# Forgetting attention and a gated convolution FFN: the second load of the gates on the sync engine's queue, and another order for the first quarter of the work

## The chip, the core and the metric

The kernel runs on one core of a Trainium2 chip. The metric is the device time of one execution in microseconds (us); the time given for the kernel is the median of several runs. A core has five engines that each work through their own list of instructions in order and wait for one another through semaphores: PE (TensorE, matmuls; its weight loads are shown as PEld), DVE (VectorE), ACT (ScalarE), POOL (GpSimd) and SP (SyncE, which here only issues DMA transfers). ACT can issue DMA transfers too; each of the two has a DMA queue of its own.

## The reference

```python
# q, k, v: (8, 8, 576, 64) = batch, heads, sequence, head dim; f: (8, 8, 576)
scores = (q @ k.T) / sqrt(64)
cum = cumsum(log(clip(f, 1e-4, 1)), axis=-1)
scores = where(causal, -1e9, scores + cum[..., :, None] - cum[..., None, :])
attn = softmax(scores) @ v
x = attn.transpose(0, 2, 1, 3).reshape(8, 576, 512)
h = relu(x @ w_in)                        # (8, 576, 1024)
conv = conv_w[0] * h[t - 1] + conv_w[1] * h[t] + conv_w[2] * h[t + 1]
out = (h * sigmoid(conv)) @ w_out         # (8, 576, 512)
```

## The kernel before

**Groups and blocks.** The 64 heads are worked in 16 groups of 4 (`hb` 0 to 15); two groups make one batch entry (`b` 0 to 7), whose feed-forward part (FFN) starts when both of its groups are through. Keys come in blocks of 128 and one of 64.

**Tasks.** Every piece of work is a named task. `Plan.add` records its engine, what it needs, and which buffers it takes and gives back; `Plan.play` emits the tasks in the order of the string `ORDER`, one name after another. That string therefore sets each engine's list: a task stands on its engine behind all tasks of that engine that are ahead of it in the string, and where a task may run on several engines, `@ACT`, `@DVE` or `@POOL` behind its name chooses. Nothing is reordered afterwards.

The names that matter here (first number: the group, the pair of heads, or the batch entry):

- `ld0.p.s`, `ld1.p.s` (L159): plain loads of q (s = 0) and k (s = 1) of groups 0 and 1; `tp` (L166): their transposes on PE, 9 each; `cl` (L172 on ACT, L174 on DVE): the copy of a transpose out of PSUM into the working tile `qk`. Its scale and bias also clear the rows between and set the constant ones that stand beside the decay rows.
- `q2.s` and on (L180): for groups 2 and later q and k are loaded by a transposing DMA, in one go per side; `cl2.s` and on (L186) then clear the rows between on DVE, up to group 7.
- `dca` (L527), `dcl` (L267), `dcs` (L271), `dck` (L274, L275): clip f, its logarithm, the running sum, and the decay rows `kc` in bfloat16, as a high and a low part. Partitions 0 to 63 hold the 64 heads, and 64 to 127 hold them again, so f is loaded twice, from L223 and L224. `ki` (L280) writes the rows to a DRAM image in three stores; `rw1` and on (L203, L204) load them from there into the tile of a group. Group 0 does not need that image: its scores add the decay with two more matmuls (L316, L318).
- `cw`, `cwt` (L295, L298 to L305): the convolution weights, transposed on PE, and their ratios.
- `sd`, `so` (L313, with L321 for the mask): the diagonal and off-diagonal scores of a pair of heads; `st`: the tail of a group; `ed`, `eo` (L354, L371), `et` (L333): their exponentials on ACT.
- `v` (L210): loads of v in five pieces per batch entry; `va` (L218, L220): the cast to float16; `pv` (L390, L395): attention times v; `n`, `m` (L404, L406): the normalisation on DVE; `t` (L415) and `tx` (L418): the transposed result `xt`.
- `wi`, `wic`, `wo`, `woc` (L511, L519): loads of w_in and w_out in four pieces each through the tiles `ob`, and their casts.
- `f` (L430): first FFN matmul of a slice of 128 features; `r` (L441): its relu on ACT; `c`, `d` (L447, L449): the two steps of the convolution on DVE; `a` (L452): the gate's tanh or sigmoid on ACT; `g` (L459): the product on DVE; `o` (L475): the second FFN matmul; `e`, `s`: its way out.

Matmuls and transposes write to four PSUM tiles in turn (`ps0` to `ps3`), so a task on PE can also wait for the engine that empties the tile that it takes.

**Queues.** All loads and stores but three are issued by SP. ACT issues the two loads of f and the load of the convolution weights (L226) at the very start. A DMA on SP waits until the one that used the same one of eight completion semaphores has landed; those show as `DMAHW0` to `DMAHW7` in the order below.

## Time and profile before

| what | us |
|---|---|
| runs shown | 249.43, 246.55, 248.5; median 248.5 |
| the profiled execution's own time | 246.53 |
| its span, first to last instruction | 244.8 |
| PE busy | 226.9 |
| DVE busy | 205.9 |
| ACT busy | 206.8 |
| POOL busy | 51.5 |

The clock that TensorE was granted is 0.999 over the span. A profile row of a group gives the engine, the line, the operation, what it writes and reads with the form, its busy time and its mean; a row of the timeline gives the start, the length, the engine and line, and in brackets how long the engine was idle before and what ended that. The chain of waits follows the work that ended last back from the end; its rows give the start, the length and who held the chain. `SPq` and `ACTq` are the engines as issuers of DMAs; such a row lasts as long as the issue, not as the transfer.

### The profile page before, as it was taken

The numbers are of one execution on the slowest core, as the hardware profiler recorded it, in microseconds if no ns is written. First come the engines' busy times: TensorE is split into PE (matmuls) and PEld (weight loads), VectorE is DVE, ScalarE is ACT, GpSimd is POOL, SyncE is SP. The second block draws the span as 40 slices with busy tenths as digits, with TensorE's granted clock in tenths as the row PEclk, the third lists the DMA queues.
The fourth block names the chain that finished last, engine by engine and source line by source line (L and its number), as shares of the span: only waits on it lengthen the run. The fifth ranks groups of instructions, "written<-read, shape, count | busy, mean of one in ns | idle before, by whom it ended". The sixth has DMA issues, their size and how long they took to land.

```text
span 244.8 us, 6395 instructions
## 1 busy us (share of the span) xinstructions
PE 226.9 (93%) x2627; PEld 145.2 (59%) x2627; DVE 205.9 (84%) x323; ACT 206.8 (84%) x278; POOL 51.5 (21%) x77
## 2 busy tenths in 40 slices
PE   0899799779989999999999999999999999999991
PEld 0787585557555676575556765685575566444440
DVE  5635359999998999999999979996999889999941
ACT  2768677999989899999999999999988996798442
POOL 8020520004220030022311580165302221000000
PEclk9999999999999999999999999999999999999999
DMA  7999999999899999999999999969997870541426
GB/s 189 333 162 243 289 212 197 196 249 260 187 178 177 222 162 246 252 297 208 195 251 264 202 189 274 263 144 186 240 255 192 210 165 3 146 162 58 163 86 214
DMA packets 120280, 49.68 MB, mean 203 GB/s; under 512 B 109863, under 2 KB 110375, under 8 KB 120251
## 3 DMA queue, kind: packets, MB, share of 16 engines
q1 hardware_dynamic: 120085, 48.97, 89.7%
q8 instruction: 20, 0.33, 0.6%
q10 hardware_dynamic: 166, 0.31, 0.4%
q14 instruction: 9, 0.07, 0.1%
HBM read 21.11 MB, written 10.17 MB: 128 GB/s over the span
## 4 chain that ended last, share of the span: by engine, by line
PE 80%; DVE 8%; DMA 6%; issue 1%; ACT 1%; POOL 1%; ACTq 1%; SPq 0%; DVEq 0%
PE ps L475 25%; PE ps L430 21%; PE ps L313 15%; PE ps L390 7%; PE ps L395 3%; PE ps L166 2%; PE ps L415 2%; PE ps L321 2%; DMA pd<-in_moe_conv_w_dram 2%; DMA ob<-in_moe_w_out_dram 2%; DVE u L447 2%; DVE u L449 2%; DMA qk<-image 2%; DVE hg L459 1%; DVE qk L186 1%
## 5 line engine op out<-in xcount | busy, mean ns | idle before, releaser
L430 PE MATMUL ps<-xt,w_in_f 128*128 128x512 f16 (+1 forms) x512 | 69.9, 286 | 0.0
L371 ACT ACTIVATE pp<-ps 128x1024 f16<-128x1024 f32 x64 | 64.8, 1033 | 4.4 <-PE ps L313 2.8
L475 PE MATMUL ps<-w_out_f,hg 128*128 128x512 f16 x288 | 66.9, 379 | 0.7 <-POOL w_out_f L519 0.7
L313 PE MATMUL ps<-qk 128*128 128x128 bf16 (+2 forms) x576 | 63.4, 240 | 1.6 <-DMA qk<-image 0.8
L447 DVE SCALAR_TENSOR_TENSOR u<-ht,cwt 128x576 f32<-128x576 f16 x64 | 53.3, 849 | 3.2 <-ACT ht L441 3.2
L452 ACT ACTIVATE hg<-u,cw 128x576 f16<-128x576 f32 x64 | 48.7, 784 | 5.9 <-DVE u L449 5.8
L449 DVE SCALAR_TENSOR_TENSOR u<-ht,cwt,u 128x576 f32<-128x576 f16 x64 | 53.1, 844 | 0.5
L430 PEld LDWEIGHTS <-w_in_f 128*128 128x128 f16 x512 | 34.4, 98 | 28.5
L313 PEld LDWEIGHTS <-qk 128*128 128x128 bf16 x576 | 39.2, 98 | 19.8 <-issue 3.0
L441 ACT ACTIVATE ht<-ps 128x576 f16<-128x576 f32 x64 | 40.9, 663 | 6.2 <-DVE hg L459 3.1
L475 PEld LDWEIGHTS <-hg 128*128 128x128 f16 x288 | 26.9, 98 | 29.7 <-issue 0.9
L459 DVE SCALAR_TENSOR_TENSOR hg<-hg,ht 128x576 f16<-128x576 f16 x51 | 39.0, 776 | 0.5 <-ACT hg L452 0.5
L357 POOL TENSOR_SCALAR_AFFINE_SELECT pp<-pd 128x1024 f16<-128x1024 f32 x16 | 19.7, 1244 | 51.7 <-ACT pd L354 51.7
L390 PE MATMUL ps<-va,pp 128*128 128x65 f16 x640 | 24.8, 193 | 1.0 <-DVE va L218 1.0
L390 PEld LDWEIGHTS <-pp 128*128 128x128 f16 x640 | 22.5, 97 | 3.5 <-DVE va L218 1.3
L406 DVE TENSOR_TENSOR xm<-ps,rc 128x896 f16<-128x896 f32 (+1 forms) x32 | 23.9, 751 | 0.5
L354 ACT ACTIVATE pp<-ps 128x1024 f16<-128x1024 f32 x16 | 16.6, 1038 | 5.2 <-PE ps L313 4.2
L354 ACT ACTIVATE pd<-ps 128x1024 f32<-128x1024 f32 x16 | 16.2, 1023 | 1.2 <-PE ps L313 1.0
L218 POOL CAST va<-vf 128x1024 f16<-128x1024 f32 x8 | 9.3, 1168 | 33.2 <-PE ps L415 18.5
L321 PE MATMUL ps<-mask,ident 128*128 128x512 bf16 (+1 forms) x40 | 14.3, 358 | 1.6 <-ACT pp L371 0.8
L404 DVE RECIPROCAL rc<-ps 128x14 f32<-128x14 f32 (+1 forms) x32 | 6.7, 209 | 9.8 <-PE ps L395 5.9
L480 ACT COPY ob<-ps 128x1024 f32<-128x1024 f32 (+1 forms) x14 | 12.9, 919 | 0.3 <-issue 0.2
(83 smaller groups left out, 176.2 us busy)
## 6 DMA issues: line engine op xcount, KB each, us to landing
vf<-in_v_dram SPq DMA_DIRECT2D x32, 256.0 KB
out_dram<-ob SPq DMA_DIRECT2D x14, 512.0 KB
qk<-blank SPq DMA_DIRECT2D x8, 432.0 KB
ob<-in_moe_w_in_dram SPq DMA_DIRECT2D x4, 512.0 KB
ob<-in_moe_w_out_dram SPq DMA_DIRECT2D x4, 512.0 KB
out_dram<-ob SPq DMA_DIRECT2D x6, 256.0 KB
vf<-in_v_dram SPq DMA_DIRECT2D x8, 128.0 KB
qk<-blank SPq DMA_DIRECT2D x8, 108.0 KB
```

Of the source, the lines that this page charges most:

```text
L313: nc.tensor.matmul(o, tk[:, h * S + k0:h * S + k0 + 128], tq[:, h * S + q0:h * S + q0 + n], start=first, stop=last and not by_matmul(hb, h))
L354: nc.scalar.activation(o, ps_of(f"sd{i}").rearrange("p (s c) -> p s c", s=2), AF.Exp, scale=SCALE)
L371: nc.scalar.activation(pair(i)[:, s, 512:1536], ps_of(f"so{i}.{s}"), AF.Exp, scale=SCALE)
L390: nc.tensor.matmul(ps[:, c:c + D + 1], block(hb, h, m, n), va[:, h, m, 0:D + 1], start=(m == 0), stop=(m == n))
L406: nc.vector.tensor_tensor(xm[:, CUT * D * u:CUT * D * u + nj * k * D].rearrange("p (j x d) -> p j x d", x=k, d=D), got[:, :, :, 0:D], r.un ...
L430: nc.tensor.matmul(ps[:, t0:t1], w_in_f16[:, cc, 128 * ff:128 * (ff + 1)], xt[:, cc // 2, x:x + t1 - t0], start=(cc == 0), stop=(cc == NCC ...
L441: nc.scalar.activation(ht_of(b, ff)[:, 2:2 + S], ps_of(f"f{b}.{ff}")[:, 0:S], AF.Relu, scale=1.0 if (b, ff) in LATE else 0.5)
L447: nc.vector.scalar_tensor_tensor(u, ht[:, 1:1 + S], cwt[:, ff, 0:1], ht[:, 2:2 + S], op0=ALU.mult, op1=ALU.add)
L449: nc.vector.scalar_tensor_tensor(u, ht[:, 3:3 + S], cwt[:, ff, 1:2], u, op0=ALU.mult, op1=ALU.add)
L452: nc.scalar.activation(hg_of(b, ff), u_t[slot[f"c{b}.{ff}", "u"]], AF.Sigmoid if (b, ff) in LATE else AF.Tanh, scale=cw[:, ff, 1:2])
L459: nc.vector.scalar_tensor_tensor(hv, hv, 1.0, ht_of(b, ff)[:, 2:2 + S], op0=ALU.add, op1=ALU.mult)
L475: nc.tensor.matmul(ps[:, 512 * (c % 2):512 * (c % 2 + 1)], w, w_out_f16[:, ff, :], start=(ff == 0), stop=(ff == NFF - 1))
```

## The change

The second load of f leaves ACT and becomes a task of SP, `lf`, which the clip `dca` now needs. The order string is new up to `a1.1`; from there on it is the same text.

```diff
     nc.scalar.dma_start(fsb[0:BH], f.rearrange("b h s -> (b h) s"))
-    nc.scalar.dma_start(fsb[BH:128], f.rearrange("b h s -> (b h) s"))
     nc.scalar.preload_act_table(AF.Ln)
     nc.scalar.dma_start(cwrow, moe_conv_w)
...
-    add("dca", "DVE", [], lambda: nc.vector.tensor_scalar(fsb, fsb, 1e-4, 1.0, op0=ALU.max, op1=ALU.min))
+    add("lf", "SP", [], lambda: nc.sync.dma_start(fsb[BH:128], f.rearrange("b h s -> (b h) s")))
+    add("dca", "DVE", ["lf"], lambda: nc.vector.tensor_scalar(fsb, fsb, 1e-4, 1.0, op0=ALU.max, op1=ALU.min))
```

The beginning of the order string, before and now:

```
-dca cw ld0 ld1 ld0.0.0 tp0.0.0 dcl ld0.1.0 ld0.0.1 tp0.0.1 tp0.1.0 v0.0 ld0.1.1 ld1.0.1 ld1.0.0 dcs dck v0.1 v0.2 v0.3 v0.4 ...
+ld0 ld1 ld0.0.1 lf ld1.0.0 ld0.0.0 cw dca tp0.0.0 dcl tp1.0.0 ld0.1.0 tp0.0.1 ld1.0.1 cl0.0.0@ACT dcs tp0.1.0 dck ld0.1.1 cl0.0.1@ACT ...
```

Lines after L224 have a number lower by one in the changed kernel, up to the new task.

SP's list at the start, before (a name's last number is the buffer):

```order
L159 DMA hg_124<-in_q_dram 128x576 x2
L159 DMA hg_124<-in_k_dram 128x576
L210 DMA vf0_89<-in_v_dram 128x8x64
L159 DMA hg_124<-in_k_dram 128x576
L159 DMA hg_124<-in_k_dram 128x2x576 [waits DMAHW0_49]
L159 DMA hg_124<-in_q_dram 128x2x576 [waits DMAHW1_49]
L210 DMA vf0_89<-in_v_dram 128x8x64 [waits DMAHW2_49]
L210 DMA vf0_89<-in_v_dram 128x8x64 [waits DMAHW3_49]
L210 DMA vf0_89<-in_v_dram 128x8x64 [waits DMAHW4_49]
L210 DMA vf0_89<-in_v_dram 64x8x64 [waits DMAHW5_49]
L180 DMA_TRANSPOSE qk2_87<-in_k_dram 128x2304 [waits DMAHW6_49]
L280 DMA image_65<-kc_73 64x576 [waits DMAHW7_49,DVE_49]
```

and now (128x576 is one pair of group 0, 128x2x576 is group 1):

```order
L159 DMA hg_124<-in_k_dram 128x576
L526 DMA u0_120<-in_f_dram 64x576
L159 DMA hg_124<-in_q_dram 128x2x576
L159 DMA hg_124<-in_q_dram 128x576 x2
L159 DMA hg_124<-in_k_dram 128x2x576
L159 DMA hg_124<-in_k_dram 128x576 [waits DMAHW0_49]
L210 DMA vf0_89<-in_v_dram 128x8x64 [waits DMAHW1_49]
L279 DMA image_65<-kc_73 64x576 [waits DMAHW2_49,DVE_49]
L279 DMA image_65<-kc_73 64x576 [waits DMAHW3_49]
L279 DMA image_65<-kc_73 64x576 [waits DMAHW4_49,DVE_49]
L180 DMA_TRANSPOSE qk2_87<-in_k_dram 128x2304 [waits DMAHW5_49]
L180 DMA_TRANSPOSE qk2_87<-in_q_dram 128x2304 [waits DMAHW6_49]
```

The f load stands second, q of group 0's first pair has gone from the first place to the fourth, and the three stores of the decay rows stand ahead of the transposing loads and of four of the five pieces of v.

ACT's list around the first relu (L441 before, L440 now; `pp` are exponentials, `ht` relus, `xt` the transposed attention), before:

```order
L354 ACTIVATE pp4_99<-ps0_129 128x2x512 [waits PE_49]
L371 ACTIVATE pp4_99<-ps2_131 128x1024 [waits PE_49]
L354 ACTIVATE pp5_100<-ps2_131 128x2x512 [waits PE_49]
L441 ACTIVATE ht0_115<-ps0_129 128x576 [waits DVE_49,PE_49]
L441 ACTIVATE ht1_116<-ps3_132 128x576 [waits DVE_49,PE_49]
L371 ACTIVATE pp5_100<-ps1_130 128x1024
L441 ACTIVATE ht2_117<-ps0_129 128x576 [waits PE_49]
L371 ACTIVATE pp4_99<-ps2_131 128x1024
```

and now:

```order
L353 ACTIVATE pp4_99<-ps2_131 128x2x512 [waits PE_49]
L417 COPY xt0_113<-ps3_132 128x1152 [waits DVE_49,PE_49]
L370 ACTIVATE pp4_99<-ps2_131 128x1024 [waits PE_49]
L353 ACTIVATE pp5_100<-ps3_132 128x2x512 [waits PE_49]
L370 ACTIVATE pp5_100<-ps1_130 128x1024 [waits DVE_49,PE_49]
L370 ACTIVATE pp4_99<-ps2_131 128x1024 [waits PE_49]
L440 ACTIVATE ht0_115<-ps3_132 128x576 [waits PE_49]
L518 CAST w_in_f16_69<-ob3_128 128x2x512 [waits DMAHW4_49]
L440 ACTIVATE ht1_116<-ps0_129 128x576 [waits DVE_49,PE_49]
```

Two exponentials have moved ahead of the first relu, a copy of xt has come from DVE, and a cast of w_in from POOL stands between the first two relus.

SP's list from the loads of groups 4 and 5 to w_out, before:

```order
L180 DMA_TRANSPOSE qk0_85<-in_q_dram 128x2304 [waits DMAHW5_49]
L180 DMA_TRANSPOSE qk1_86<-in_q_dram 128x2304 [waits DMAHW6_49,PE_49]
L180 DMA_TRANSPOSE qk1_86<-in_k_dram 128x2304 [waits DMAHW7_49]
L511 DMA ob0_125<-in_moe_w_out_dram 128x2x512 [waits DMAHW0_49,Pool_49]
L203 DMA qk0_85<-image_65 1x2304 [waits DMAHW1_49,DVE_49]
L204 DMA qk0_85<-image_65 2x2304 [waits DMAHW2_49]
L511 DMA ob1_126<-in_moe_w_out_dram 128x2x512 [waits DMAHW3_49,Pool_49]
L511 DMA ob2_127<-in_moe_w_out_dram 128x2x512 [waits DMAHW4_49,Pool_49]
```

and now:

```order
L180 DMA_TRANSPOSE qk0_85<-in_k_dram 128x2304 [waits DMAHW4_49,PE_49]
L180 DMA_TRANSPOSE qk0_85<-in_q_dram 128x2304 [waits DMAHW5_49]
L180 DMA_TRANSPOSE qk1_86<-in_k_dram 128x2304 [waits DMAHW6_49,PE_49]
L180 DMA_TRANSPOSE qk1_86<-in_q_dram 128x2304 [waits DMAHW7_49]
L510 DMA ob0_125<-in_moe_w_out_dram 128x2x512 [waits DMAHW0_49,Pool_49]
L203 DMA qk0_85<-image_65 1x2304 [waits DMAHW1_49,DVE_49]
L204 DMA qk0_85<-image_65 2x2304 [waits DMAHW2_49,DVE_49]
L510 DMA ob2_127<-in_moe_w_out_dram 128x2x512 [waits DMAHW3_49,Pool_49]
L510 DMA ob3_128<-in_moe_w_out_dram 128x2x512 [waits DMAHW4_49,Activation_49]
L510 DMA ob1_126<-in_moe_w_out_dram 128x2x512 [waits DMAHW5_49,Pool_49]
```

Before, k of group 4 had been loaded ahead of v and group 3's decay rows (L203, L204), and w_out's fourth piece came after the next five pieces of v; now the four loads of groups 4 and 5 stand in a row behind those decay rows, and all of w_out follows at once.

2 lines of the change are left out of this document (1 added, 1 removed).

## The prediction

> **What bounds the kernel now.** First the page's share of busy time, then the same by stage, because a mean over the span hides where TensorE (PE) waits.
>
> ```profile
> span 244.8 us, 6395 instructions
> PE 226.9 (93%) x2627; PEld 145.2 (59%) x2627; DVE 205.9 (84%) x323; ACT 206.8 (84%) x278; POOL 51.5 (21%) x77
> ```
>
> The busy time of the engines in stretches (start:end, length, then PE, weight loads, VectorE, ScalarE and GpSimd, each with its count):
>
> ```profile
> 25.00:37.00 12.00, 10.45 (x186) 8.12 (x183) 4.51 (x11) 8.40 (x10) 5.15 (x5) 1.00 1.12 247
> 37.00:60.00 23.00, 19.79 (x271) 13.21 (x270) 22.77 (x34) 21.45 (x31) 2.29 (x3) 1.00 1.08 230
> 60.00:75.00 15.00, 14.33 (x121) 8.25 (x119) 14.65 (x19) 13.85 (x20) 3.97 (x4) 1.00 1.00 185
> 75.00:227.00 152.00, 151.98 (x1784) 94.79 (x1781) 141.59 (x213) 140.45 (x195) 33.34 (x33) 1.00 0.89 199
> ```
>
> From 75 to 227 us PE never pauses (151.98 of 152) while DVE and ACT idle 10 to 12 us each. The order there is the same before and after, so the end moves by what PE has gained when it comes to the place where the two orders join, provided the others keep up. All that can be won is PE's idle time before it: 12.00 - 10.45 = 1.55, 23 - 19.79 = 3.21 and 15 - 14.33 = 0.67 us, 5.4 in all, plus a part of the 8.3 us before the first transpose. The chain of waits names what ended each:
>
> ```profile
> 2.06 5.13 DMA pd<-in_moe_conv_w_dram
> 7.32 0.98 PE ps L295 x8
> 8.31 3.91 PE ps L166 x36
> ...
> 15.30 0.50 PE ps L166 x9
> ...
> 17.11 0.50 PE ps L166 x9
> 17.61 0.22 PE ps L321
> ...
> 19.39 1.00 PE ps L166 x18
> ...
> 22.51 3.80 DMA qk<-image
> ...
> 36.96 0.76 DVE xt L418
> 37.72 1.45 DVE qk L186 x2
> 39.23 0.83 DVE u L447
> ...
> 47.68 0.60 DVE va L218
> ...
> 64.27 5.08 DMA ob<-in_moe_w_out_dram
> ...
> 71.14 1.02 PE ps L475 x4
> ```
>
> At the start it is a load; at 22.5 to 26.3 us the decay rows of group 1 (L203/L204); from 37 us DVE, which is busy 22.77 of 23 us up to 60; at 64 to 71 us the last piece of w_out.
>
> **The change part by part.** *The gate load.* Before, both halves of f go through ACT's queue, the conv weights behind them. What the two queues moved from 2.4 to 6 us, and then in all from 6 to 12:
>
> ```profile
> DMA packets 502, 1.00 MB, mean 279 GB/s; under 512 B 67, under 2 KB 67, under 8 KB 502
> ...
> q1 hardware_dynamic: 340, 0.71, 76.9%
> q10 hardware_dynamic: 162, 0.30, 26.7%
> ```
>
> ```profile
> DMA packets 2579, 2.02 MB, mean 336 GB/s; under 512 B 1909, under 2 KB 1909, under 8 KB 2579
> ```
>
> Queue q10 is ACT's (f and conv weights are 0.3 MB), q1 is SP's. After the change the second half of f (0.147 MB) stands second in q1 behind k of pair 0 (0.295 MB). With the first half on q10 that makes 0.59 MB; at 279 GB/s from 2.4 us this is 2.1 us, so f is there at about 5 us. VectorE's clip waits for it:
>
> ```profile
> 6.59 0.46 DVE L527 TENSOR_SCALAR u<-u 128x576 f32<-128x576 f32 x1 [2.32 <-DMA u<-in_f_dram]
> ...
> 9.69 0.76 DVE L275 SCALAR_TENSOR_TENSOR kc<-u,kc 64x576 bf16<-64x576 f32 x1
> ```
>
> So the decay rows are ready 1.5 us sooner, at 9.0 instead of 10.45. By itself this is worth nothing: the first scores wait for transposed q and k as well.
>
> *The first transposes.* The conv weights get ahead of half of f, so PE's L295 no longer holds the first transpose; q of pair 0 does, now fourth in q1. Ahead of it and with it lie 0.295 + 0.147 + 0.590 + 0.295 = 1.33 MB, and 0.16 on q10: 1.49 MB, which is 5.3 us at 279 GB/s and 4.4 at 336, thus 6.8 to 7.7 us; I take 7.4 against 8.31, a gain of 0.9. If q1 kept the rate that it had beside q10 (0.71 MB in 3.6 us, 197 GB/s) it would be 9.1, a loss of 0.8.
>
> The Trainium skill (DMA: Bandwidth & Descriptors, section Queues, rings and completion order) says that each DMA engine takes turns between the queues that have work, packet by packet. By that rule q1 gets the whole rate as soon as f's one half on q10 is through, and 7.4 is more likely than 9.1; the 162 packets of q10 beside 340 of q1 fit it.
>
> *From there to the convolution.* PE in the new order: four slow transposes from 7.4 (3.9 us as in the x36 row) to 11.3; the first diagonal scores after ACT's copy of the third transpose (10.3, and 1.25 a copy by the L172 row below), 11.6 to 13.4 (17.61 to 19.39 gives 1.8 each); two transposes, 1.0; off-diagonal scores (15.80 to 17.11, 1.3) to 15.7; two transposes to 16.7; diagonal to 18.5; the tail scores, 1.3 by these rows (22.85 to 24.20), to 19.8:
>
> ```profile
> 22.85 0.27 PE L321 MATMUL ps<-mask,ident 128*128 128x256 bf16 x1
> ...
> 24.20 1.16 PE L390 MATMUL ps<-va,pp 128*128 128x65 f16 x32
> ```
>
> From here ACT sets the pace. Its rows:
>
> ```profile
> 9.42 3.71 ACT L172 ACTIVATE qk<-ps,lim 128x1152 uint16<-128x1152 uint16 x3 [0.35 <-PE ps L166]
> ...
> 27.23 1.02 ACT L354 ACTIVATE pp<-ps 128x1024 f16<-128x1024 f32 x1 [2.44 <-PE ps L313]
> 28.15 1.02 ACT L371 ACTIVATE pp<-ps 128x1024 f16<-128x1024 f32 x1
> ...
> 38.46 0.65 ACT L441 ACTIVATE ht<-ps 128x576 f16<-128x576 f32 x1 [0.98 <-PE ps L430]
> ...
> 56.93 1.12 ACT L418 COPY xt<-ps 128x1152 f16<-128x1152 f16 x1
> ```
>
> One large exponential each 0.92 us. The 2.44 us in which ACT waited for group 1's scores go: the new order issues the decay rows about 18 to 19 us instead of 22 to 23, ahead of the w_in loads, and even at 3.80 us to landing they are there by 23, when PE wants them. Between the tail and the first relu the new order has 16 large exponentials (14.7), two tails (0.3 each, a quarter of the columns) and a copy of xt that was DVE's (1.1): 19.8 + 16.4 = 36.2. The last transpose, DVE's copy (0.76) and the first FFN matmuls lie partly beside ACT's last exponentials and add an estimated 1.1: the first relu at 37.3 against 38.46. So DVE's first convolution (39.23) comes **1.2 us** earlier. ACT has by then also done two exponentials that stood behind the first relu before; that 1.8 us of lead counts only where ACT is the bound.
>
> *From the convolution to the join.* DVE does the same work up to there, less a copy of xt (0.76), plus a cast of v (0.60): **0.1 us** less, rounded down. It has little idle time to absorb a late operand, and one is possible: a cast of w_in, GpSimd's before, now stands on ACT between the first two relus. I cost that at nothing, because DVE has the second half of the first convolution to do and ACT has 1.8 us of lead; without that cover it would be about one exponential, 0.9.
>
> *w_out.* All four pieces are loaded and cast before SP's second loads of v. PE's wait for the last falls away, **0.7 us**:
>
> ```profile
> PE ps L475 <- POOL w_out_f L519: 0.7, 1, 0.7
> ```
>
> The row is of the waits (total, times, longest).
>
> *What may take it back.* The loads. SP issues back to back up to the join, so a faster compute stage does not make them faster:
>
> ```profile
> 16.59 2.35 SPq L280 DMA_DIRECT2D image<-kc  x3
> ...
> 42.14 7.18 SPq L180 DMA_TRANSPOSE qk<-in_q_dram  x2
> 49.36 2.28 SPq L180 DMA_TRANSPOSE qk<-in_k_dram  x1
> ...
> 52.38 0.26 SPq L203 DMA_DIRECT2D qk<-image  x1
> ...
> 76.18 3.18 SPq L180 DMA_TRANSPOSE qk<-in_k_dram  x1
> ```
>
> ```profile
> 81.59 1.66 DVE L186 TENSOR_SCALAR qk<-qk,lim 128x2304 uint16<-128x2304 uint16 x2
> ```
>
> The last transposed load before the join is issued until 79.36, and DVE takes it at 81.59 without a wait, so it lands in between. DVE would now want it at 80.2: a loss between 0 and 1.4, I take **0.7** (the middle; no row says which).
>
> Sum: -1.2 - 0.1 - 0.7 + 0.7 = **-1.3 us**. The profiled execution took 246.53 us (its span of 244.8 and 1.7 around it) and lies at the lower end of the runs shown; I predict the median, 248.5 - 1.3 = **247.2 us**. Its own range: with the start 0.6 us earlier than taken (6.8) and the load for nothing, 245.9; with the start 1.7 later (9.1), 248.9.
>
> **The rivals.** *ACT sets the pace of 37 to 60 us, not DVE.* For it: ACT is busy 21.45 of 23 us and PE's waits there are for ACT as well as DVE. Against: DVE is fuller. Then the lead is 1.2 + 1.8 = 3.0, and with the 0.7 for w_out 3.7: 244.8 us.
>
> *The load queue falls behind (slower).* SP's third kind of work, the three image stores, now stands ahead of the transposed loads of groups 2 and 3, and waits for the decay rows until 9.0. What was issued before it, 2.9 MB, is through by 11 to 13 us, and the next large load cannot be issued before 9.0 + 2.35 = 11.3. In the middle the four transposed loads of groups 4 and 5 come in one row behind group 3's decay rows, which wait for DVE's two clamps (37.72 before, 1.45; now done by about 37.8). With those and a piece of v they start at about 40. At 3.15 us each (the mean of the three from 42.14 to 51.64) they end at 52.6, at the slowest pace there, 3.6, at 54.4, against 51.64 before, and group 4's decay rows (52.38) come 1 to 3 us later. The first I have costed at nothing: by the 3.80 us to landing they are there at about 57.5, when PE reaches group 4's scores. At the second PE waits for group 4's scores and what hangs on them, and the join is 2.7 us later than before rather than 1.3 earlier: 251.2 us. It decides from the point where SP ends the last of these four loads after 54 us. Against it: the pieces of w_out, which took SP's queue at 64 us before, are out of the way then.
>
> *The loads set the pace exactly.* DVE waits for the last load its full 1.4, and PE's 0.7 is lost in DVE's wait: no change, 248.5.
>
> *PE's clock.* 36 transposes took 109 ns each and later ones 56: PE is slow in its first 4 to 5 us. In the new order it does the conv weights at about 5 us, pauses, and starts again at 7.4. If the pause costs a further 3.4 us at half speed, 1.7 us are lost: 248.9.
> The Trainium skill (TensorE: Matmul & The Clock Gate, Part 1) gives such a rule: half the clock until a window of about 3.4 us was busy. The trace agrees (full speed 3.9 us after 8.31); a run of the change alone shows where the window falls.
>
> **How the numbers follow.** Forecast 0.42, ACT's pace 0.25, late loads 0.20, loads exact 0.08, clock 0.05. A measurement of this kernel can tell about 1%, 2.5 us, from no change (its three runs spread 246.55 to 249.43). Faster by over that: ACT's pace and a small part of the forecast, 0.30. Slower: late loads, 0.20. Within: 0.50. The range of 8 in 10 runs from below ACT's pace to the late loads: 243.9 to 251.1.
>
> **What would show it.** The clip of f near 5 us and the first L166 near 7.4 (over 8.3: my order of arrivals is wrong). No DMA wait of PE at 22 to 26 us, ACT without the 2.44. The first relu at 37.3, the first L447 at 38; if these are right and the end is not, the loads or DVE took it: an L186 with a wait for a DMA between 70 and 82. No wait of L475 for GpSimd. SP's last of the four transposed loads of groups 4 and 5 before 54 us. A PE that pauses more than 4 us between 25 and 75 would prove me wrong.

## The result, and the profile after

The changed kernel takes 250.49 us (median of 20 runs, 248.41 to 252.52) against 247.25 (20 runs, 245.96 to 250.83): a ratio of 1.0113, interval 1.0088 to 1.0137. It is slower by 1.1%, about 3 us, where 1.3 us faster was predicted. The profiled execution took 252.26 us and lies at the upper end of its runs, so the same kernel was traced a second time (span 247.1 us, below), and of the run with group 5's decay rows later, whose traced execution took 272.93 us, no trace is read; what only the first trace shows is said to be so.

The page of the changed kernel, share of busy time:

```profile
span 250.6 us, 6392 instructions
PE 229.2 (91%) x2627; PEld 145.8 (58%) x2627; DVE 209.4 (84%) x325; ACT 208.2 (83%) x279; POOL 50.0 (20%) x74
```

The same stretches as in the prediction (the first two and the fifteen us behind them):

```profile
25.00:37.00 12.00, 11.59 (x204) 9.10 (x203) 4.47 (x10) 11.17 (x13) 3.06 (x3) 1.00 1.11 235
37.00:60.00 23.00, 20.35 (x278) 13.55 (x275) 20.70 (x33) 21.54 (x30) 1.48 (x2) 1.00 1.02 189
60.00:75.00 15.00, 12.10 (x109) 7.07 (x108) 14.96 (x16) 11.46 (x16) 6.99 (x5) 1.00 0.97 222
```

PE's idle time from 25 to 37 us has indeed gone (11.59 of 12 busy, 10.45 before). From 60 to 75 us it has grown (12.10 of 15 busy, 14.33 before), while DVE is full, with 16 instructions (18 in the second trace) in the time of 19, and GpSimd is busy 6.99 us instead of 3.97. That points at longer instructions on DVE, which its timeline below confirms. The start, in the chain of waits (start, length, who held it):

```profile
2.49 6.86 DMA hg<-in_q_dram
9.40 3.07 PE ps L166 x27
12.49 1.32 ACT qk L172
13.86 0.59 PE ps L320
...
16.42 1.02 PE ps L166 x18
```

The first transposes begin at 9.40 us, 1.1 later than before, and a load of q holds them. The decay side is early, as the timeline of DVE has it (the clip of f, the decay rows):

```profile
5.32 0.46 DVE L527 TENSOR_SCALAR u<-u 128x576 f32<-128x576 f32 x1 [1.04 <-DMA u<-in_f_dram]
...
8.41 0.76 DVE L274 SCALAR_TENSOR_TENSOR kc<-u,kc 64x576 bf16<-64x576 f32 x1
```

DVE in its timeline from 62 to 70 us, and GpSimd beside it:

```profile
62.09 1.59 DVE L448 SCALAR_TENSOR_TENSOR u<-ht,cwt,u 128x576 f32<-128x576 f16 x1
63.60 0.81 DVE L446 SCALAR_TENSOR_TENSOR u<-ht,cwt 128x576 f32<-128x576 f16 x1
...
65.12 1.59 DVE L448 SCALAR_TENSOR_TENSOR u<-ht,cwt,u 128x576 f32<-128x576 f16 x1
...
68.81 1.59 DVE L446 SCALAR_TENSOR_TENSOR u<-ht,cwt 128x576 f32<-128x576 f16 x1
```

```profile
61.80 1.28 POOL L518 CAST w_out_f<-ob 128x1024 f16<-128x1024 f32 x1 [14.61 <-DMA ob<-in_moe_w_out_dram]
64.55 1.56 POOL L518 CAST w_out_f<-ob 128x1024 f16<-128x1024 f32 x1 [1.47 <-DMA ob<-in_moe_w_out_dram]
66.91 2.88 POOL L518 CAST w_out_f<-ob 128x1024 f16<-128x1024 f32 x2 [0.80 <-DMA ob<-in_moe_w_out_dram]
```

A step of the convolution takes 0.81 us when GpSimd rests and 1.59 when one of its casts runs beside it; the cast too is longer (1.28 to 1.56, before at best 1.04). The kernel before has the same effect in a few places, as these rows of DVE and GpSimd show (the second cast runs beside the step):

```profile
70.22 1.47 DVE L449 SCALAR_TENSOR_TENSOR u<-ht,cwt,u 128x576 f32<-128x576 f16 x1
...
56.43 1.04 POOL L519 CAST w_out_f<-ob 128x1024 f16<-128x1024 f32 x1 [13.69 <-DMA ob<-in_moe_w_out_dram]
...
69.40 1.69 POOL L519 CAST w_out_f<-ob 128x1024 f16<-128x1024 f32 x1 [2.00 <-DMA ob<-in_moe_w_out_dram]
```

DVE's rows grouped (count, busy time and mean, idle time ahead), from the first convolution step to that of slice 3 of the second batch entry (71.62 us before, 76.80 after), first before and then after:

```profile
L447 DVE SCALAR_TENSOR_TENSOR u<-ht,cwt 128x576 f32<-128x576 f16 x12 | 10.8, 915 | 0.3 <-ACT ht L441 0.3
L449 DVE SCALAR_TENSOR_TENSOR u<-ht,cwt,u 128x576 f32<-128x576 f16 x11 | 9.5, 880 | 0.1
L459 DVE SCALAR_TENSOR_TENSOR hg<-hg,ht 128x576 f16<-128x576 f16 x8 | 5.7, 747 | 0.0
```

```profile
L446 DVE SCALAR_TENSOR_TENSOR u<-ht,cwt 128x576 f32<-128x576 f16 x11 | 11.2, 1023 | 0.0
L448 DVE SCALAR_TENSOR_TENSOR u<-ht,cwt,u 128x576 f32<-128x576 f16 x11 | 10.6, 968 | 0.7 <-DVE u L446 0.5
L458 DVE SCALAR_TENSOR_TENSOR hg<-hg,ht 128x576 f16<-128x576 f16 x8 | 6.7, 853 | 0.0
```

At 0.81 us for a convolution step and 0.75 for a product, the time over the plain one is 26.0 - (23 x 0.81 + 8 x 0.75) = 1.4 us before and 28.5 - (22 x 0.81 + 6.0) = 4.7 after.

SP's rows of the changed kernel from group 4's decay rows on:

```profile
57.70 0.26 SPq L203 DMA_DIRECT2D qk<-image  x1
58.06 0.60 SPq L204 DMA_DIRECT2D qk<-image  x1
58.76 1.59 SPq L510 DMA_DIRECT2D ob<-in_moe_w_out_dram  x3
60.40 0.46 SPq L210 DMA_DIRECT2D vf<-in_v_dram  x1
65.23 0.24 SPq L203 DMA_DIRECT2D qk<-image  x1
65.53 0.57 SPq L204 DMA_DIRECT2D qk<-image  x1
66.15 3.60 SPq L210 DMA_DIRECT2D vf<-in_v_dram  x4
69.86 7.60 SPq L180 DMA_TRANSPOSE qk<-in_q_dram  x2
77.51 5.90 SPq L180 DMA_TRANSPOSE qk<-in_k_dram  x2
```

SP stands from 60.9 to 65.2 us: group 5's decay rows (`rw5`, L203) wait for DVE's clamp. The row of SP's waits from 40 to 90 us (line waited for, total, times, longest):

```profile
SPq L203 <- DVE qk L186: 4.5, 2, 4.3
```

The four transposed loads of groups 6 and 7 start at 69.86, before at 64.7. DVE then takes the last of them, with the clamp that stood at 81.59 us before:

```profile
83.33 0.88 DVE L186 TENSOR_SCALAR qk<-qk,lim 128x2304 uint16<-128x2304 uint16 x1 [0.47 <-DMA qk<-in_k_dram]
85.94 1.66 DVE L186 TENSOR_SCALAR qk<-qk,lim 128x2304 uint16<-128x2304 uint16 x2
```

This pair of clamps (call it the **last clamp**) turned out to be the best marker of all: in 19 traces of this study the span ends 162.7 to 164.7 us behind its start (median 163.1), whatever was changed ahead of it. It is reached by two ways. By the compute way it follows PE's second output tile of the first batch entry (the **join**; 72.44 us before, 76.42 after) by 9.15 to 9.6 us. By the load way it cannot start before k of group 7 has landed.

### The profile page after: what moved, and what is told of

Its sections match the earlier page's. It is cut to its first block, busy times and chain, and to the rows that moved or that the text cites. A ratio compares the mean times of both kernels' runs of the same rounds, so it can differ in the third digit from the quotient of the medians.

```text
span 250.6 us, 6392 instructions
## 1 busy us (share of the span) xinstructions
PE 229.2 (91%) x2627; PEld 145.8 (58%) x2627; DVE 209.4 (84%) x325; ACT 208.2 (83%) x279; POOL 50.0 (20%) x74
## 4 chain that ended last, share of the span: by engine, by line
PE 68%; DVE 10%; ACT 7%; DMA 7%; SPq 4%; issue 2%; ACTq 0%; DVEq 0%
PE ps L474 24%; PE ps L429 17%; PE ps L312 12%; PE ps L389 6%; ACT pp L370 3%; DVE u L446 3%; DMA hg<-in_q_dram 3%; SPq L180 2%; DMA qk<-in_q_dram 2%; DVE u L448 2%; PE ps L394 2%; PE ps L166 2%; DMA qk<-image 2%; DVE hg L458 2%; PE ps L414 2%
## 5 line engine op out<-in xcount | busy, mean ns | idle before, releaser
L446 DVE SCALAR_TENSOR_TENSOR u<-ht,cwt 128x576 f32<-128x576 f16 x64 | 54.7, 869 | 2.9 <-ACT ht L440 2.9
L448 DVE SCALAR_TENSOR_TENSOR u<-ht,cwt,u 128x576 f32<-128x576 f16 x64 | 54.2, 861 | 1.1 <-DVE u L446 0.5
L440 ACT ACTIVATE ht<-ps 128x576 f16<-128x576 f32 x64 | 41.2, 660 | 8.0 <-DVE hg L458 6.0
L458 DVE SCALAR_TENSOR_TENSOR hg<-hg,ht 128x576 f16<-128x576 f16 x51 | 40.3, 800 | 0.3 <-ACT hg L451 0.3
L218 POOL CAST va<-vf 128x1024 f16<-128x1024 f32 x7 | 8.6, 1228 | 34.2 <-PE ps L312 20.1
```

The costliest lines, as they stand in the source:

```text
L440: nc.scalar.activation(ht_of(b, ff)[:, 2:2 + S], ps_of(f"f{b}.{ff}")[:, 0:S], AF.Relu, scale=1.0 if (b, ff) in LATE else 0.5)
L446: nc.vector.scalar_tensor_tensor(u, ht[:, 1:1 + S], cwt[:, ff, 0:1], ht[:, 2:2 + S], op0=ALU.mult, op1=ALU.add)
L448: nc.vector.scalar_tensor_tensor(u, ht[:, 3:3 + S], cwt[:, ff, 1:2], u, op0=ALU.mult, op1=ALU.add)
L458: nc.vector.scalar_tensor_tensor(hv, hv, 1.0, ht_of(b, ff)[:, 2:2 + S], op0=ALU.add, op1=ALU.mult)
```

## The experiments

Three causes were set against each other. **START**: the first transposes come late, and with them the first convolution. **CAST**: GpSimd's casts of w_out, now beside the convolution, stretch DVE's steps. **LOADS**: SP's transposed loads come late, the prediction's slower rival. Where the expectations say k or q of pairs 4, 6 and 7, the transposed loads of groups 4, 6 and 7 are meant. All runs in one table (first transpose, first convolution step, join, last clamp with its wait for k of group 7, span; of each run's trace, in us; the ratio is of its runs to the kernel before on the same chip, with its interval; it is not the quotient of the medians, from which it differs by up to 0.4%):

| kernel | first L166 | first step | join | last clamp | span | ratio |
|---|---|---|---|---|---|---|
| before | 8.3 | 39.23 | 72.44 | 81.59 | 244.8 | 1 |
| changed | 9.40 | 41.60 | 76.42 | 85.94 | 250.6 | 1.0113 (1.0088 to 1.0137) |
| changed, second trace | 9.08 | 40.65 | 74.54 | 83.86 | 247.1 | 1.0102 (1.0032 to 1.0171) |
| moved load alone | 6.29 | 39.71 | 72.38 | 81.74 | 244.9 | 0.9964 (0.9939 to 0.9989) |
| q first | 6.18 | 39.54 | 74.89 | 84.53 | 247.8 | 1.0077 (1.0037 to 1.0116) |
| w_out casts on ACT | 9.00 | 40.53 | 75.08 | 84.24 | 247.4 | 1.0056 (1.0030 to 1.0081) |
| rows of group 5 later | | | | | | 1.0104 (1.0068 to 1.0140) |
| casts cut | 8.94 | 40.52 | 71.83 | 84.42, 1.12 | 248.7 | 1.0090 (1.0059 to 1.0121) |
| q first, casts cut | 6.81 | 39.37 | 71.15 | 83.14, 1.08 | 245.8 | 1.0039 (1.0015 to 1.0062) |
| moved load alone, casts cut | 6.82 | 39.49 | 72.32 | 81.48 | 244.6 | 0.9966 (0.9937 to 0.9995) |
| moved load alone, casts of v on GpSimd | 6.31 | 40.13 | 74.70 | 83.86 | 247.0 | 1.0014 (0.9993 to 1.0035) |
| q first, casts cut, rows of group 5 later | 7.02 | 38.44 | 74.91 | 84.07 | 247.2 | 1.0090 (1.0046 to 1.0134) |
| q first, rows of group 5 later | 5.97 | 39.70 | 75.02 | 84.17 | 247.5 | 1.0071 (1.0035 to 1.0108) |
| q first, casts on ACT, rows later | 6.58 | 38.84 | 74.02 | 83.18 | 246.3 | 1.0068 (1.0030 to 1.0105) |
| q first, casts cut, k of group 4 early | 6.82 | 39.78 | 73.75 | 85.99, 1.10 | 248.7 | 1.0085 (1.0047 to 1.0122) |
| k of group 4 early | 9.41 | 40.94 | 78.57 | 87.73 | 250.9 | 1.0233 (1.0180 to 1.0286) |
| q first, casts on ACT, k of group 4 early | 6.11 | 38.14 | 75.67 | 84.83 | 247.9 | 1.0124 (1.0078 to 1.0170) |
| q first, casts cut, k of group 6 second | 6.81 | 38.24 | 69.50 | 81.25, 2.51 | 244.0 | 1.0014 (0.9975 to 1.0053) |
| q first, casts on ACT, k of group 6 second | 5.99 | 39.33 | 74.12 | 83.28 | 246.4 | 1.0065 (1.0035 to 1.0096) |
| q first, k of group 6 second | 5.91 | 38.69 | 73.48 | 84.93, 2.17 | 247.6 | 1.0103 (1.0052 to 1.0155) |

Each row of times is of one execution. In eight of these traces the clock that TensorE was granted fell for a stretch: to 0.89 from 60 to 75 us with q first, alone and in the two runs that add later rows of group 5 to it without the casts on ACT; to 0.86 from 25 to 37 us with the moved load alone and with casts of v on GpSimd, and in the latter to 0.83 from 50 to 60; less, or elsewhere, in three others. If PE were busy all through, 11% of 15 us would be 1.6 us, an estimate from these figures; so a difference of about 1 us between two such times need not be the edit's.

**The moved load alone.** The order of before, with the second load of f on SP:

```diff
-dca cw ld0 ld1 ld0.0.0 tp0.0.0 ...
+cw ld0 ld1 ld0.0.0 lf dca tp0.0.0 ...
```

> The order of before; only the second load of f moves to SP, behind the first load of q. Three theories of why the change is slower. START: in the changed kernel q of the first pair stands fourth in SP's queue, the first transpose comes at 9.40 us instead of 8.31 and PE's clock rises later, so DVE's first convolution is 2.4 us late. CAST: in the changed kernel more and longer casts of GpSimd fall on DVE's convolution steps, which then take 1.59 instead of 0.81 us, so DVE loses about 2.7 us in the middle. LOADS: the decay rows and transposed loads of groups 4 to 7 come later in SP's order. All three say that the moved load alone is harmless: within 0.4% of before, with the conv weights about 1 us earlier and the first transpose at 7 to 8 us. If moving the load is itself what costs, this is slower than before by over 0.7%.

Measured: 246.58 us, 0.9964 (by the medians, 246.58 against 246.94, only 0.9985). The load does no harm and at most a little good; everything lost is lost by the order.

**q of pair 0 first.** The changed kernel, with its first loads and transposes in another order, rest kept:

```diff
-ld0 ld1 ld0.0.1 lf ld1.0.0 ld0.0.0 cw dca tp0.0.0 dcl tp1.0.0 ld0.1.0 tp0.0.1 ld1.0.1
+ld0 ld1 ld0.0.0 lf ld0.0.1 cw dca ld0.1.0 ld1.0.0 tp0.0.0 dcl tp0.0.1 tp1.0.0 ld1.0.1
```

> The changed kernel, but q and k of the first pair are loaded first (f between them) and transposed first, then q of group 1; the rest of the order is the changed one. START expects the first transpose at 6.5 to 7.5 us instead of 9.4, DVE's first convolution at 39.2 to 39.8 instead of 41.6, and most of the loss back: 0.8% to 1.0% less time than the changed kernel, so a ratio to before of 1.001 to 1.004. CAST expects that DVE is held up later all the same: 1.006 to 1.009. LOADS expects no change: 1.009 to 1.013.

Measured: 249.87 us, 1.0077. The first convolution step is back at 39.54, but the join is not (74.89). START is at most a part; in time alone the two kernels are not told apart, since the interval overlaps that of the changed kernel. Of the 2.9 us by which the first transposes come sooner than in the second trace (6.18 against 9.08), only 1.1 arrive at the first convolution step, because PE soon waits for another load of q:

```profile
9.07 2.10 PE L166 MATMUL ps<-ident_b,hg 128*128 128x128 bf16 x18 [0.80 <-DMA hg<-in_q_dram]
```

**The w_out casts on ACT.**

```diff
-... woc1@POOL ... woc2@POOL ... woc0@POOL ... woc3@POOL ...
+... woc1@ACT ... woc2@ACT ... woc0@ACT ... woc3@ACT ...
```

> The changed kernel with the four casts of w_out on ACT instead of GpSimd, at the same places of the order. CAST expects that DVE's steps of 1.59 us between 60 and 70 us shrink to 0.81, about 3 us of DVE, while ACT takes on 4 x 0.92 = 3.7 us in a stretch where it was 11.46 of 15 us busy: 0.5% to 1.0% less than the changed kernel, a ratio to before of 1.001 to 1.006. START and LOADS expect nothing or a loss from the fuller ACT: 1.010 to 1.020.

Measured: 248.9 us, 1.0056, the one single edit that wins back time clear of noise (its interval, 1.0030 to 1.0081, lies below that of the changed kernel). DVE's steps from 60 to 70 us are 0.81 us again, and now ACT is full, 15.00 of 15 us:

```profile
60.00:75.00 15.00, 12.15 (x102) 6.92 (x101) 13.79 (x19) 15.00 (x21) 1.35 (x1) 1.00 1.04 207
```

CAST holds, but its price is not read cleanly here: four casts of 1.1 us have been put on an engine that was busy 11.46 of these 15 us before.

**Group 5's decay rows later,** behind the loads of v, so that SP does not stand for DVE's clamp:

```diff
-... v2.0 rw5 v2.1 v2.3 v2.2 v2.4 ...
+... v2.0 v2.1 v2.3 v2.2 v2.4 rw5 ...
```

> The changed kernel with the decay rows of group 5 behind the five second loads of v in SP's list, as before, so that SP does not stand at 60.9 to 65.2 us waiting for DVE's clamps. LOADS expects the transposed loads of groups 6 and 7 3 to 4 us sooner (first issue at 66 instead of 69.9) and a ratio to before of 1.003 to 1.008. START and CAST expect at most 0.2% of the time back: 1.009 to 1.013.

Measured: 249.56 us, 1.0104: nothing, as START and CAST had it.

**The casts cut.** They copy 16 of 1024 columns, so GpSimd does next to nothing there and ACT no more than before. The rest of w_out is left out of the product; a memset on DVE (1.8 us, at the start) fills it with zeros:

```diff
+    nc.vector.memset(w_out_f16, 0.0)
...
+        if w == "wo":
+            dst, ob = dst[:, :, 0:8], ob[:, :, 0:8]
```

> The changed kernel, whose four casts of w_out copy 16 of 1024 columns each, so that GpSimd works next to nothing beside VectorE's convolution from 60 to 75 us (the rest of w_out stays zero: part of the second FFN product is left out; loads and all matmuls stay). Theory CAST (GpSimd's casts double VectorE's convolution steps): the four steps of 1.59 us beside them fall to 0.81, VectorE and with it the join is up to 3.1 us earlier in the trace, and because ACT, unlike in the run with the casts on ACT, has no more to do, more comes back than there: 247.8 to 248.4 us, ratio to before 1.002 to 1.005. Rival START (only the late first transpose counts): 250 us, ratio 1.010 as before.

Measured: 248.99 us, 1.0090, in time not told apart from the uncut kernel, where 1.002 to 1.005 was expected. Yet the trace does what CAST said: the join is at 71.83, 2.7 us earlier than in the second trace of the uncut kernel and even ahead of the kernel before. From the first convolution step to the join it is 31.3 us, against 34.8 and 33.9 in the two traces of the uncut kernel and 33.2 before the change. What comes then is a new wait: DVE stands 2.28 us for k of group 6 and 1.12 for k of group 7, and the last clamp is at 84.42. The gain was made and given back to the loads within 13 us.

**q first and casts cut,** the two edits above together.

> The changed kernel with both suspected costs taken away: loads and first transposes in the order that starts PE at 6.2 us, and the four casts of w_out cut to 16 of 1024 columns (part of w_out is left out). If START and CAST are all there is: 1.0113 less 0.0036 less about 0.008, ratio 0.998 to 1.001, about 247 us, with the first convolution step at 39.5 us and the join near 72.2. If a third cause sits in the order of the middle (rival LOADS: SP's later transposed loads, or the order of the tasks themselves): the ratio stays at 1.005 or more, and PE or VectorE show idle time between 40 and 75 us that ends on a DMA.

Measured: 247.81 us, 1.0039, between the two outcomes; its interval (1.0015 to 1.0062) lies apart from that of the changed kernel, so the two edits together win back more than half of the loss. Idle time that ends on a DMA is there, as the second outcome had it, but behind the join and not between 40 and 75 us. DVE's timeline, then the chain of waits through the same place:

```profile
79.37 0.88 DVE L186 TENSOR_SCALAR qk<-qk,lim 128x2304 uint16<-128x2304 uint16 x1 [1.28 <-DMA qk<-in_k_dram]
83.14 1.67 DVE L186 TENSOR_SCALAR qk<-qk,lim 128x2304 uint16<-128x2304 uint16 x2 [1.08 <-DMA qk<-in_k_dram]
```

```profile
71.31 1.73 PE ps L475 x8
73.53 2.85 SPq L180
76.43 6.68 DMA qk<-in_k_dram
83.14 1.67 DVE qk L186 x2
```

The chain leaves PE at 73 us and runs through SP's issue of the last load and its 6.68 us of transfer. The join is at 71.15, 1.3 us before the old one, and the last clamp still 1.55 us after the old one. So LOADS is real once the other two are taken away; in the changed kernel it stood behind or level with them.

**The control: the cut and the moved load in the order of before,** again two edits shown above.

> The control: the order of before with the moved load alone, and the same cut of the four w_out casts to 16 of 1024 columns (part of w_out is left out). There the casts meet fewer of VectorE's steps: by the trace the convolution and gate steps between the first step and the join took 1.1 us over their plain 0.81 and 0.75 in the kernel before, 4.6 us in the changed one. CAST expects a gain of about 1 us over the moved load alone, ratio 0.991 to 0.994, smaller than the gain of the same cut in the changed kernel (2 to 2.7 us). If the cut is worth the same in both orders, the casts are not what tells the orders apart.

Measured: 246.13 us, 0.9966, no gain over the moved load alone (0.9964): my 1 us did not come, though in the trace DVE's steps are plain again. In that order the stretched steps cost nothing that shows: the join moves from 72.38 to 72.32, and PE waits 1.4 us for a cast of v where it waited 1.0. My reading is that a stretched step costs only where DVE is the last to end. By the test as I had set it (the same worth of the cut in both orders) the times of the two cuts alone do not tell the orders apart; their joins do, 2.7 us in the new order and 0.06 in the old.

**The converse: the two casts of group 3's v on GpSimd,** in the order of before with the moved load:

```diff
-va3.0@ACT ... va3.1@ACT
+va3.0@POOL ... va3.1@POOL
```

> The converse: the order of before with the moved load alone, but the two casts of group 3's v (about 1.1 and 0.4 us on ACT) on GpSimd, as in the changed kernel. CAST: VectorE sets the pace there, one or two more of its steps are stretched by 0.8 us each: 0.8 to 1.6 us slower than the moved load alone, ratio 1.000 to 1.003. Rival (ACT sets the pace of that stretch): ACT is relieved of 1.5 us, so it is faster by up to 1.5 us, ratio 0.990 to 0.996. If neither: 0.9964.

Measured: 247.41 us, 1.0014, 0.5% slower than without (0.9964, taken on another chip), as CAST said and against the rival by which ACT, relieved of 1.5 us, would be faster. Its executions had a lower granted clock (0.990 in the mean, 0.995 without the edit); those at 0.993 or more still have a mean of 247.0 us, 0.3 above the kernel before at such a clock, where the moved load alone is 0.4 below. DVE's two steps beside the cast take 2.46 us instead of 1.54, and its own cast of v behind them, for which PE waits 2.1 us instead of 1.0, comes at 49.44 instead of 48.10 (0.4 us of that were there at the first step). That its join is 2.3 us later is not the casts' alone, since TensorE's clock fell to 0.83 from 50 to 60 us in this trace:

```profile
47.06 2.46 DVE L448 SCALAR_TENSOR_TENSOR u<-ht,cwt,u 128x576 f32<-128x576 f16 x2
49.44 0.88 DVE L218 CAST va<-vf 128x1024 f16<-128x1024 f32 x1
```

**The changed kernel again.**

> The changed kernel once more, for a second trace beside the first, whose profiled execution lay at the upper end of its runs. All theories: ratio 1.009 to 1.014. What the trace tells: whether the first transpose near 9.4 us, TensorE's slow stretch up to 16 us, the convolution steps of 1.59 us beside GpSimd's casts, and VectorE's wait for the transposed k of the last pair at 83 us come again. START expects the first relu at 39.5 to 41, CAST 3 to 5 us of stretched steps between 43 and 75 us.

Measured: 249.49 us, 1.0102; first transpose 9.08, first step 40.65, last clamp 83.86. The stretched steps come again (28.3 us for 31 steps, counted as above 3.7 over the plain ones); TensorE was at full speed at 13.5 us, where the first trace has it from 15.2 on, and DVE did not wait for a load at 81 or 84 us. TensorE's longer slow stretch and that wait were thus seen in one of the two traces only. Of the 3.7 us some 2.4 lie beside casts of w_out (62.5 to 67.2 us) and 1.4 beside casts of v (43.6 to 46.0 and 70.1 to 71.5), so the casts of v on GpSimd are a part of CAST that my name for it left out.

**Three runs on SP's rows of group 5,** the edit that puts `rw5` behind v2.4 added to others shown above. With q first and the casts cut:

> The changed kernel with the start in the order that begins PE at 6.2 us, with the w_out casts cut to 16 of 1024 columns (part of w_out is left out), and with group 5's decay rows issued behind the loads of v, so that SP is not held 58 to 62 us by VectorE's clamp. With the first two alone the ratio was 1.0039, and VectorE waited 1.3 and 1.1 us for the transposed k of pairs 6 and 7 at 79 to 83 us. LOADS behind the two others: SP issues the last of those loads near 76.3 us instead of 79.4, VectorE's wait and PE's idle 2 us from 75 to 100 go, ratio 0.994 to 0.998. If the loads are not the cause: 1.004 again.

Measured: 249.34 us, 1.0090, neither outcome, and worse by 0.5% if at all (the intervals overlap). The edit does not do what LOADS expected of it. The loads of v hold SP by themselves (8.75 us for the five, as 8.68 in the kernel before), the decay rows go out at 65.55 instead of 62.36, and PE waits for them (line waited for, total, times, longest):

```profile
PE ps L313 <- DMA qk<-image: 3.7, 2, 3.6
```

With q first and the casts left whole, and with the casts on ACT:

> The same start and the same later decay rows of group 5, but the w_out casts whole and on GpSimd (nothing is left out). CAST: VectorE's stretched steps keep the join near 74.9 us, which hides the loads, so the later decay rows are worth 0.5 us at most beside the start alone (1.0077): 1.005 to 1.008. LOADS as a cause of its own, at work beside the casts: 1.000 to 1.003.

> The whole repair, nothing left out: the start in the order that begins PE at 6.2 us, the four w_out casts on ACT, group 5's decay rows behind the loads of v. START (0.0036), CAST (0.0057) and LOADS together: 0.996 to 1.001. ACT, whose 1.1 us a cast comes on top of 29.4 us from the first convolution step to the join, then sets that stretch, so it does not reach the run with the casts cut. If the order of the middle has a further cost of its own: 1.003 or more.

Measured: 248.85 us, 1.0071, as CAST said; and 248.87 us, 1.0068, the second outcome and not the repair that I hoped for: ACT is again busy all 15 us from 60 to 75.

**Three runs on k of group 4.** It is loaded ahead of the second loads of v, as before the change; first with q first and the casts cut, then alone, then with q first and the casts on ACT:

```diff
-... v1.0 v1.2 ... v1.1 ... v1.3 rw3 v1.4 q4.1 q4.0 ...
+... q4.1 v1.0 v1.2 ... v1.1 ... v1.3 rw3 v1.4 q4.0 ...
```

> The changed kernel with the earlier start, the w_out casts cut to 16 of 1024 columns (part of w_out is left out), and the transposed load of k of pair 4 issued ahead of the second loads of v, as in the kernel before (there at 34.5 us, in the changed kernel at 43.4, behind group 3's decay rows). Without this last edit the ratio was 1.0039, with VectorE waiting 1.3 and 1.1 us for the transposed k of pairs 6 and 7. LOADS as the third cause (SP stands one transposed load, 3.3 us, behind from 43 us on): the last four loads begin 2 to 3 us earlier than 66.3, VectorE does not wait, PE idles under 0.5 us from 75 to 100: ratio 0.994 to 0.999. Rival (the rate at which the queue drains sets the last loads, whatever the order): they land at the same time, 1.003 to 1.005.

> The changed kernel with that one load moved alone, nothing left out. If LOADS is a cause of its own, as the rival of the prediction had it: 1.003 to 1.007. If the start and the stretched steps hide it: 1.009 to 1.013, as without the move.

> Nothing left out: the earlier start, the four w_out casts on ACT, k of pair 4 issued early. If the three causes are all there is: 0.997 to 1.002. If the order of the middle costs something further, or ACT with its four casts sets the pace of 60 to 75 us: 1.004 to 1.007, as with the later decay rows in the place of the early load (1.0068).

Measured: 1.0085 (249.15 us), 1.0233 (252.65) and 1.0124 (249.97). The second is worse by another 1.2% than the changed kernel. The first overlaps its neighbour without the move (1.0039), and the third has none, since q first with the casts on ACT was not run without a further edit. None came out as LOADS had it: that SP is simply one load behind is not borne out. The load pushes the next loads of v back, and the cast of v stands on DVE, ahead of its next steps; what DVE waited for in the first of these from 20 to 75 us (4.2 us in all without the move):

```profile
DVE va L218 <- DMA vf<-in_v_dram: 5.9, 2, 3.6
```

**Three runs on the order of the last four loads,** k of group 6 second as before the change; first with q first and the casts cut, then with q first and the casts on ACT, then with q first alone:

```diff
-... q6.0 o0.0 q7.0 q6.1 q7.1 ...
+... q6.0 o0.0 q6.1 q7.0 q7.1 ...
```

> As the run with the earlier start and the cut casts (1.0039; part of w_out is left out), but of the last four transposed loads k of pair 6 goes second, as before the change, and q of pair 7 third. If the order of these four is what VectorE waits for: its wait for k of pair 6 (1.3 us) goes, that for k of pair 7 (1.1 us) stays or shrinks: 1.000 to 1.003. If it is the time at which the four begin: 1.004, the wait merely standing at pair 7.

Measured: 247.94 us, 1.0014, not to be told from the kernel before. The wait for k of group 6 went; the whole of it came back at group 7, as the second theory had it:

```profile
81.25 1.67 DVE L186 TENSOR_SCALAR qk<-qk,lim 128x2304 uint16<-128x2304 uint16 x2 [2.51 <-DMA qk<-in_k_dram]
```

Its join, 69.50 us, is 2.9 us ahead of the kernel before, its last clamp 0.3. Whether the order of the four or an earlier `rw5` (60.72 us here, 62.36 without the swap) brought the clamp forward these two runs do not tell; the intervals of 1.0014 and 1.0039 overlap.

> Nothing left out: the changed kernel with the earlier start, the four w_out casts on ACT, and k of pair 6 second among the last four transposed loads, the order that with the casts cut gave 1.0014. If the three causes are all there is and ACT can carry the casts: 0.999 to 1.003. If ACT with its four casts (4.4 us) sets the pace of 60 to 75 us: 1.004 to 1.007, with the join near 74 us and VectorE not waiting for k of pairs 6 and 7.

> The same with the casts back on GpSimd, nothing left out. If the casts are what remains: the join near 74.5 us by VectorE's stretched steps, the order of the last loads hidden behind it, 1.005 to 1.008 as with the start alone (1.0077). If the order of the last loads is a cause of its own: 1.001 to 1.004.

Measured: 248.43 us, 1.0065 with the casts on ACT (join 74.12, no wait for either k, ACT 15.00 of 15 us from 60 to 75: its second outcome); 249.38 us, 1.0103 with the casts on GpSimd, neither outcome, though the interval (1.0052 to 1.0155) reaches into the first. In the latter the load way was the later one, against my expectation that the casts would hide it:

```profile
84.93 1.67 DVE L186 TENSOR_SCALAR qk<-qk,lim 128x2304 uint16<-128x2304 uint16 x2 [2.17 <-DMA qk<-in_k_dram]
```

**What follows from all of them.** Where DVE waits for k of group 7 at the last clamp, that clamp comes 20.5 to 21.4 us after `rw5` was issued (60.72 to 81.25, 62.36 to 83.14, 63.05 to 84.42, 64.97 to 85.99, 63.92 to 84.93): four loads of v and four transposed loads stand between. Before the change it was 18.5 us (63.09 to 81.59) without a wait; there all five loads of v stood ahead of the rows, and a piece of w_out behind them. Now both ways can be worked out for the changed kernel. First trace: compute 76.42 + 9.2 = 85.6, loads 65.23 + 20.5 to 21.4 = 85.7 to 86.6; measured 85.94. Second trace: 74.54 + 9.2 = 83.7, loads 63.30 + 20.5 to 21.4 = 83.8 to 84.7; measured 83.86. In neither trace did the last clamp wait for k of group 7, so that load had landed 20.7 and 20.6 us after `rw5` at the latest: compute decided there (in the first trace with the 0.5 us for k of group 6), and if these loads took no less than the 20.5 us seen elsewhere, they landed within 0.2 us of it. **The two ways end together, each some 2 to 4 us later than before.** This fits that no repair of one of them alone brought the time back. The loads are in part bound to the casts as well, because `rw5` waits for a clamp on DVE: with q first it goes out 2.2 us later with the casts whole than cut (64.53 and 62.36), and with k of group 6 second 3.2 (63.92 and 60.72); with the late start it is only 0.25 (63.30 in the second trace, 63.05), because there the stretched steps beside w_out come behind the clamp. No kernel with the new order and nothing left out came back to the time before (1.0056 at best), and where the casts went to ACT, ACT was full; so that the three causes are all there is, is not shown. The version that beats both is the old order with the moved load, 0.9964, by little.

## Why the prediction was wrong, point by point

Two terms of the sum failed, and a third was mis-sized. The start was to gain 1.2 us and lost 1.4; DVE's work up to the join was to take 0.1 us less and took 1.9 more; and the loads, taken as fixed in time, came later with the compute side instead of costing 0.7 by themselves.

- *Decay rows at 9.0, clip near 5:* right (9.17 and 5.32). From 17 to 38 us no wait of PE is for a DMA either; ACT's 2.44 us went, and 2.5 and 1.8 us for the late transposes and scores took their place in the first trace. The first relu came at 40.83 and 39.89 us instead of 37.3, and PE's pauses from 25 to 75 us add up to 6.0 and 5.1, over the 4 that were to prove the prediction wrong.
- *First transposes at 7.4:* **failed**; 9.40 and 9.08, at the bound of 9.1 that I had and did not take. The estimate counted the 1.49 MB that stand ahead of q of pair 0 and with it. From the start to 9.4 us 2.20 MB were moved:

```profile
DMA packets 1054, 2.20 MB, mean 234 GB/s; under 512 B 101, under 2 KB 101, under 8 KB 1054
...
q1 hardware_dynamic: 968, 2.04, 71.3%
q10 hardware_dynamic: 86, 0.16, 4.8%
```

  So 0.7 MB of loads issued behind q moved before it had landed. The rate was as taken (294 GB/s from 2.4 to 9.4 us, the prediction had 279 to 336); the amount was not. Being fourth in the queue did not mean that only three were served before. That the bound of 9.1 comes out near is luck: it supposed q1 held at 197 GB/s by q10, and q1 moved 1.90 MB of the 2.06 in these 7 us. The rule of the Trainium skill that I weighed (DMA: Bandwidth & Descriptors, section Queues, rings and completion order) was about two queues; q10 had few packets here, 86, and so the conclusion from it missed what went on inside q1.
- *From the first transpose to the convolution in 30.6 us:* 32.2 in the first trace and 31.6 in the second; with q early, 31.4 (6.81 to 38.24) in the best. 1.0 to 1.6 us too short as a length. With the late start the first step is at 41.60 and 40.65 instead of 38.0: 1.4 us lost in the second trace (2.4 in the first) where 1.2 were to be gained. Of that miss of 2.6 us in the second trace the late transposes are 1.7 and the length 1.0.
- *DVE does the same work up to the join, less 0.1:* **failed**, and this is the larger loss against the kernel before, though the start missed its forecast by more (2.6 us against 2.0). The instructions are the same but for a copy and a cast, their durations are not. In the second trace the same step behind the join (71.62 before, 74.93) comes 34.3 us after the first convolution step, before 32.4: 1.9 us more, and the stretched steps, 3.7 us against 1.4, account for it. I read the row means of before (0.91 and 0.88 us) without asking why a step of 0.81 had a mean of 0.9. The prediction looked for what GpSimd's casts of w_out would spare PE and never asked whom they run beside. The cast of w_in on ACT, put at nothing, cost DVE 0.5 us at most: so long it stands behind its first step in both traces (0.1 before), though the rows name DVE itself as what it waited for.
- *w_out, 0.7 gained:* the wait of PE is gone, as said; what it was worth is not separated from the 1.2 us that PE gains on DVE in the sum below.
- *The last transposed load, 0.7 lost:* the term stood at the right place and was costed as if the compute side were on time (its 80.2 us leaves out the 0.7 of w_out; by its own sum DVE would want the load at 79.6). That SP issues back to back up to the join did not hold: SP stood 4.3 and 4.0 us for DVE's clamp, and the last load was issued until 83.41 and 79.88 instead of 79.36. In the first trace DVE's waits show 0.5 us for k of group 6, in the second none, with the compute side as late; with the casts cut they are 1.1 to 2.5 us.
- *Rival "the load queue falls behind", 251.2:* its time came nearly true, its place did not. The four loads of groups 4 and 5 ended at 56.96, behind its 54 us, in the first trace; in the second they ended before 53.9, and PE did not wait for group 4's rows (1.4 us in the first), though the kernel was as slow. The loads that counted were the next four. *PE's clock:* the first trace has a longer slow stretch, up to 15.2 us, the second not. *ACT's pace:* the control on v's casts speaks against it in the old order; in the new one ACT was full only where it was given four more casts.

Sum of the second trace: +1.4 at the start and +1.9 on DVE make DVE's step near the join 3.3 us later (74.93 against 71.62). PE does the join tile 1.2 us earlier with respect to it (0.39 ahead of it, before 0.82 behind), so the join is 2.1 us later, the last clamp 2.3 and the end of the span 2.3.

## What to carry to other kernels

Before moving work onto an idle engine, look at what the busy engine does at that time, and at the spread of durations of one and the same instruction: here a mean above the shortest was a neighbour's doing. When a chain is shortened, find the next wait that ends at nearly the same time; here one instruction, the last clamp, showed both ways, and a gain counted only as far as it moved that. Take the bytes ahead in a queue as a lower bound for a landing, not as an estimate: here 2.20 MB had moved where 1.49 were counted.

## What was not expected of the hardware

A DVE instruction with two inputs in SBUF took 1.59 us beside a GpSimd cast instead of 0.81, and that cast 1.28 to 1.56 instead of 1.04; it looks as if the two waited for one another in turn, which no run here shows directly. The clamp, which has one input, took 1.59 instead of 0.87 in the same place (62.91 us with q first). The Trainium skill (SBUF — State Buffer, section Who interferes with whom) states it: a DVE instruction with two SBUF inputs contends with a GpSimd instruction that reads SBUF; the ports that the two share are an exclusive lock. The runs agree: 0.78 us more for one step, and none with the casts on ACT, where all steps from 60 to 68 us are 0.81. It could have been read before, and with the step of 1.47 us at 70.22 in the kernel before it would have priced a cast beside the convolution at some 0.7 us.

TensorE's full speed came late in one trace and not in the next, with the same order: a mask matmul of 512 columns took 0.59 us at 13.86 in the first (0.38 at full speed), and in the second:

```profile
9.08 3.91 PE L166 MATMUL ps<-ident_b,hg 128*128 128x128 bf16 x36 [3.61 <-DMA hg<-in_q_dram]
13.54 0.38 PE L320 MATMUL ps<-mask,ident 128*128 128x512 bf16 x1 [0.55 <-ACT qk L172]
```

By the Trainium skill (TensorE: Matmul & The Clock Gate, Part 1) the speed rises after a window of about 3.4 us that was busy; the second trace agrees (3.9 us of transposes), and in the first, with the same 36 transposes in 4.0 us, it was not there 4.5 us after the first transpose; it came at 15.2 us, 5.8 after it. Why the two differ, no run here shows.
